# Attention with two kinds of heads and a maxout MLP on one Trainium2 core: both bias tables of the next head pair are made at the first chunk of the running pair

## The chip, the cores and the metric

The kernel runs on one core of one Trainium2 chip. The time is device microseconds of one execution. Before the change three runs gave 203.79, 204.90 and 205.48 us, with a median of 204.9 us. The execution that was profiled took 203.79 us; its span, from the first to the last instruction, is 202.0 us. TensorE had its full granted clock (1.000) all along.

The names of the engines in the profile: PE is TensorE (PEld its weight loads), DVE is VectorE, ACT is ScalarE, POOL is GpSimd, SP is SyncE, which issues nearly all DMAs here.

## The reference, cut to what matters

There are 4 batches, 8 heads, 768 positions and a head dimension of 64. Some heads ("retrieval") see every earlier position, the others see only the first 4 positions and a window of the last 64. Which is which comes as an input, `is_retrieval`. The output of the attention goes through an MLP that takes the larger of two products.

```python
scores = (1 / sqrt(64)) * q @ k.T                    # per batch and head
causal = rel >= 0                                    # rel = query position - key position
stream = causal & ((key < n_sink) | (rel < window))  # n_sink 4, window 64
mask   = causal where is_retrieval else stream       # per head
a      = softmax(where(mask, scores, -1e9))
x      = (a @ v), heads side by side                 # [4 * 768, 512]
out    = maximum(x @ w1, x @ w2) @ w_out             # d_ff 1024, output float32
```

## The kernel before, in words

**Tiling.** Two heads make a pair, and there are 4 pairs in a batch, 16 in all, numbered `n`. The scores are computed transposed, keys on the partitions. Of the 6 x 6 blocks of 128 x 128, the 21 on and below the diagonal of the causal mask are grouped in six chunks `c` (`CHUNKS`), four blocks each, but for chunk 3, which has one. A step `t` is one chunk of one pair: `n, c = divmod(t, 6)`.

**A chunk's way.** `scores(t)` lets PE multiply k by q into a PSUM tile `ps` (L279). `expo(t)` lets ACT take the exponential of both heads' blocks at once (L305), into `at`. `weighted(t)` lets PE multiply `at` by the values into `po` (L342). After chunk 1 and after chunk 5 half of the queries are complete, and `normalise` lets DVE take a reciprocal (L358) and multiply (L359) into `x`. There are two `ps` tiles, so the scores of a chunk wait until the exponential two chunks earlier is done.

**The bias tables.** Blocks near the diagonal need the mask. In the first batch (pairs 0 to 3) the mask is added to the scores: `scores` issues, after the q-k products of chunks 0 to 3, two more matmuls per chunk, one a head, that multiply the identity by a table `msk[:, h]` (L294), accumulating into `ps`. The table of head `h` is 128 x 512 bf16, and one DVE instruction makes it (`biases(h)`, L556, a scalar_tensor_tensor: `tab_a * rbig[h] + tab_n`). Its inputs are ready before the first pair starts, and nothing later overwrites what it reads. Once the first batch is over, `masks` turns the eight tables into tables of 0 and 1 (L563), and the later batches multiply the exponentials by them (L323, L327).

**Who transposes q and k.** For pair `n + 1`, the cast q and k are transposed on PE (L203, into a PSUM tile `pt`) during pair `n`: q in step 0, its PSUM tile copied to SBUF by ACT (L156); k in step 1, copied by DVE (L154, `qkt<-pt`). In step 3 the finished `x` of pair `n - 1` is transposed and copied by DVE (L154, `xt<-pt`). GpSimd casts q, k and v from float32 (L243, L189) and multiplies v by the retrieval flags (L191); then it makes half of the weight difference `w1 - w2` (L551), as soon as the DMA of `w1` has landed. DVE makes the other half after the first batch's scores.

**Order.** The schedule is written out by hand: each engine executes its instructions in the order in which the program issues them. The loop of the first batch issues, in step `t`: the scores and the exponential of step `t + 2`, the weighted sum of step `t - 1` (with `normalise` where a half is complete), side work, then the bias tables, then the pending transposes (`flush`). So the scores of the first chunk of pair `n + 1` are issued in step 4 of pair `n`; `normalise(n - 1, 1)` in step 0; the copy of k in step 1; `normalise(n, 0)` in step 2.

**After the first batch** come the MLP's first products, `relu(x @ (w1 - w2))` (L378; the kernel uses max(a, b) = b + relu(a - b)), then three more batches of attention with the MLP of the batch before mixed in by a planner (`fill`, `step`), which counts estimated TensorE time only while the program is being written. `biases` adds 0.7 to a count of DVE work, `given["v"]`, that is set to zero after the first batch. The last MLP ends the kernel (L378, L395).

Of the kernel before, what the change touches and what calls it, by code (L numbers as in the profile page):

```python
# [37 lines left out]
def kernel(  # L38
# [16 lines left out]
    HP = H // 2  # L55
# [82 lines left out]
    def vec(us):  # L138
        given["v"] += us
        return nc.vector  # L140
# [83 lines left out]
    def turn_half(n, half, bank, on_vector=True):  # L224

        b, p = pairs[n]
        w = S // 2
        pt = bank("pt").bitcast(BF16)[:, 0:w]
        for i in range(NB // 2):
            nc.tensor.transpose(  # L230
                pt[:, i * 128:(i + 1) * 128],
                st[n]["x"][:, half * NB // 2 + i].rearrange("p h d -> p (h d)"), ident,
            )
        evac(xts[b][:, p, half * w:(half + 1) * w], pt, 200, on_vector=on_vector)
# [30 lines left out]
    def scores(t):  # L265
        n, c = divmod(t, NCH)
        s = st[n]
        ps = psum_s.tile([128, 2, 512], F32, tag="ps", name="ps")
        runs = []
        for e, (j, i) in enumerate(CHUNKS[c][0]):  # L270
            if runs and runs[-1][0] == j and runs[-1][1] + runs[-1][3] == i:
                runs[-1][3] += 1
            else:
                runs.append([j, i, e, 1])
        w = len(CHUNKS[c][0])
        for j, i, e, m in runs:
            for hh in range(2):
                rows = slice(64 * hh, 64 * hh + 64)
                nc.tensor.matmul(  # L279
                    ps[:, hh, e * 128:(e + m) * 128],  # L280
                    lhsT=s["qkt"][rows, 1, j * 128:(j + 1) * 128],
                    rhs=s["qkt"][rows, 0, i * 128:(i + m) * 128],
                    start=(e == 0), stop=(e + m == w), skip_group_check=True,
                )
        if n < HP and CHUNKS[c][1] is not None:

            e, m, block, reps = CHUNKS[c][1]
            per = m // reps
            for hh in range(2):
                nb = msk[:, 2 * pairs[n][1] + hh, block:block + per, :]  # L290
                nb = nb.rearrange("p e c -> p (e c)")
                if reps > 1:
                    nb = nb.unsqueeze(1).to_broadcast([128, reps, per * 128])
                nc.tensor.matmul(  # L294
                    ps[:, hh, e * 128:(e + m) * 128], lhsT=ident, rhs=nb,
                    start=False, stop=True, skip_group_check=True,
                )
        s["ps", c] = ps

    def expo(t):  # L300
        n, c = divmod(t, NCH)
        s = st[n]
        w = 128 * len(CHUNKS[c][0])
        at = atp.tile([128, 2, 4, 128], BF16, tag="at", name="at")
        sca(0.13 + 2 * w / 1300).activation(  # L305
            out=at.rearrange("p h e c -> p h (e c)")[:, :, 0:w],
            in_=s["ps", c][:, :, 0:w], func=ACT.Exp, scale=scale,
        )
        s["at", c] = at

    def mask(t):
        n, c = divmod(t, NCH)
        what = CHUNKS[c][1]
        if what is None or n < HP:
            return
        e, m, at_block, reps = what
        h0 = 2 * pairs[n][1]
        at = st[n]["at", c][:, :, e:e + m, :]
        per = m // reps
        mk = msk[:, h0:h0 + 2, at_block:at_block + per, :]  # L320
        eng = vec(0.1 + m * 0.15)
        if reps == 1:
            eng.tensor_tensor(out=at, in0=at, in1=mk, op=ALU.mult)  # L323
        else:
            mk = mk.rearrange("p h e c -> p h (e c)").unsqueeze(2)
            at = at.rearrange("p h (g e) c -> p h g (e c)", g=reps)
            eng.tensor_tensor(  # L327
                out=at, in0=at, in1=mk.to_broadcast([128, 2, reps, per * 128]), op=ALU.mult
            )

    def weighted(t):
        n, c = divmod(t, NCH)
        s = st[n]
        at = s["at", c]
        for hh in range(2):
            for e, (j, i) in enumerate(CHUNKS[c][0]):
                half, col = divmod(i, 3)
                first = ("po", half) not in s
                if first:
                    s["po", half] = psum_o.tile([128, 2, 3, D + 1], F32, tag="po", name="po")  # L340
                rhs = s["vb"][:, hh, j, :] if i - j < 2 else s["vf"][:, hh, j, :]
                nc.tensor.matmul(  # L342
                    s["po", half][:, hh, col, :], lhsT=at[:, hh, e, :], rhs=rhs,
                    start=first, stop=(c == (LO_DONE, HI_DONE)[half]),
                    skip_group_check=True,
                )
        if c == LO_DONE:
            normalise(n, 0)
        if c == HI_DONE:
            normalise(n, 1)  # L350
# [79 lines left out]
    def spend(us):  # L430
        plan["pe"] += us
# [59 lines left out]
    def flush():  # L491
        while turns:
            run_short(turns)
# [55 lines left out]
    def diff_w(eng, e):  # L549
        cols = slice(e * QC, (e + 1) * QC)  # L550
        eng.tensor_tensor(  # L551
            out=w12[:, :, cols], in0=w1f[:, :, cols], in1=w2f[:, :, cols], op=ALU.subtract
        )

    def biases(h):
        vec(0.7).scalar_tensor_tensor(  # L556
            out=msk[:, h].rearrange("p e c -> p (e c)"), in0=tab_a, scalar=rbig[:, h:h + 1],
            in1=tab_n, op0=ALU.mult, op1=ALU.add,
        )
# [69 lines left out]
    def side(t, last, first_batch):  # L629

        n, c = divmod(t, NCH)
        b, p = pairs[n]
        m = n + 1
        if m < min(last, LONG):
            if c == (QS if first_batch else 0):
                turns.append((0.34, lambda bank: turn(m, 0, bank), 0))
            if c == (KS if first_batch else 1):
                turns.append((0.34, lambda bank: turn(m, 1, bank), 0))
        if m + 1 < last:
            if m + 1 < LONG and c == 5:  # L640
                cast_qk(m + 1, 0, nc.gpsimd if first_batch else nc.vector)
                cast_qk(m + 1, 1, nc.gpsimd)
            if m + 1 >= LONG and c == 2:
                cast_qk(m + 1, 0, nc.gpsimd)
                cast_qk(m + 1, 1, nc.gpsimd)
        if first_batch:
            if c == XS and n > 0:
                turns.append((0.34, lambda bank: turn(n - 1, None, bank), 0))
        elif c == (0 if p == 0 else 4) and n > HP:
            turn_x(n - 1)  # L650
        if m + 1 < last and m + 1 >= LONG and c == 4:
            turn_qk(m + 1)
        if c == 2 and m < last:
            cast_v(m, nc.gpsimd)
        if b > 0:
            if p == 0 and n > HP and c == 0 and n + 3 < len(pairs):
                load_pair(n + 3)
            if p < HP - 1 and c == 4 and n + 4 < len(pairs):
                load_pair(n + 4)
# [7 lines left out]
    for t in range(T0):  # L667
        if t + 2 < T0:
            scores(t + 2)
            expo(t + 2)  # L670
            spend(0.8)
        if t > 0:
            weighted(t - 1)
            spend(0.4)
        if t + 1 < T0:
            mask(t + 1)
        side(t, HP, True)
        n, c = divmod(t, NCH)
        if c in (1, 2) and n + 1 < HP:
            biases(2 * n + c + 1)  # L680
        flush()
        if t == 18:
            diff_w(nc.gpsimd, 0)
            diff_w(nc.gpsimd, 2)
        if t == 21:
            turn_half(HP - 1, 0, bank_d)
            diff_w(vec(1.2), 1)
# [11 lines left out]
    n = HP  # L699
# [43 lines left out]
    for t in range(T0, T + 2, 2):  # L743
# [12 lines left out]
        c = t % NCH  # L756
# [70 lines left out]
```

## Time and profile before

| what | us |
|---|---|
| median of three runs (lowest, highest) | 204.9 (203.79, 205.48) |
| the profiled execution | 203.79 |
| its span | 202.0 |
| PE busy / ACT busy / DVE busy / POOL busy | 184.6 / 113.8 / 109.5 / 67.6 |
| chain that ended last, share of the span: PE / ACT / DVE / DMA | 70% / 10% / 9% / 6% |
| first batch of attention, start of the first exponential to start of the first MLP product | 9.16 to 36.52 |
| bias tables (L556), 8 instructions, shortest / median / longest | 0.744 / 1.026 / 1.974 |

The profile is that of one execution. Its page gives the busy time of each engine, then the chain of work that ended last, and the groups of instructions by source line. The trace behind it gives each instruction with its start and duration, and for an engine's idle time what ended it. A busy PE says little by itself, since its matmuls are pipelined and their ends are modelled; the waits and the chain say what holds the time.

Shares over the whole span hide that the kernel has stages. PE is 91% busy over the span, but in the second and third pairs' stretches, 15.64 to 22.95 and 22.95 to 30.93 us, it was busy 5.83 us of 7.31 and 5.82 of 7.98; ACT was busy 5.78 and 5.77 in them, and DVE 4.88 and 5.57.

### The profile page before, as it was taken

The numbers are of one execution on the slowest core, as the hardware profiler recorded it, in microseconds if no ns is written. First come the engines' busy times: TensorE is split into PE (matmuls) and PEld (weight loads), VectorE is DVE, ScalarE is ACT, GpSimd is POOL, SyncE is SP. The second block draws the span as 40 slices with busy tenths as digits, with TensorE's granted clock in tenths as the row PEclk, the third lists the DMA queues.
The fourth block names the chain that finished last, engine by engine and source line by source line (L and its number), as shares of the span: only waits on it lengthen the run. The fifth ranks groups of instructions, "written<-read, shape, count | busy, mean of one in ns | idle before, by whom it ended". The sixth has DMA issues, their size and how long they took to land.

```text
span 202.0 us, 4508 instructions
## 1 busy us (share of the span) xinstructions
PE 184.6 (91%) x1844; PEld 103.8 (51%) x1869; DVE 109.5 (54%) x207; ACT 113.8 (56%) x153; POOL 67.6 (33%) x75
## 2 busy tenths in 40 slices
PE   7889768999789999979899999999999999999992
PEld 2356445667445555546446455555555645554440
DVE  1864593987657557478493847573733631432110
ACT  2598677578787785794536547926353622341111
POOL 1397368999005352424361533070200000000000
PEclk9999999999999999999999999999999999999999
DMA  6999999999943949999999999992704104100222
GB/s 209 298 290 335 387 351 303 324 328 305 220 73 75 201 110 220 223 197 232 198 256 216 212 233 230 207 185 97 170 2 124 73 0 143 55 0 0 104 104 104
DMA packets 82694, 37.35 MB, mean 185 GB/s; under 512 B 71794, under 2 KB 77938, under 8 KB 82674
## 3 DMA queue, kind: packets, MB, share of 16 engines
q1 hardware_dynamic: 82528, 36.77, 78.2%
q10 hardware_dynamic: 146, 0.30, 0.6%
q8 instruction: 14, 0.23, 0.5%
q14 instruction: 6, 0.05, 0.1%
HBM read 25.46 MB, written 6.29 MB: 157 GB/s over the span
## 4 chain that ended last, share of the span: by engine, by line
PE 70%; ACT 10%; DVE 9%; DMA 6%; issue 3%; SPq 0%; ACTq 0%
PE pout L395 27%; PE ph L378 19%; PE po L342 8%; PE ps L279 8%; ACT at L305 8%; DMA qkt<-qk 3%; PE pw L534 3%; PE pt L203 3%; DMA kn<-in_k_dram 2%; PE ps L294 2%; DVE msk L556 2%; DVE x L359 2%; DVE qkt L154 1%; DVE at L327 1%; ACT qkt L156 1%
## 5 line engine op out<-in xcount | busy, mean ns | idle before, releaser
L305 ACT ACTIVATE at<-ps 128x1024 bf16<-128x1024 f32 x96 | 83.5, 917 | 33.9 <-PE ps L279 28.1
L378 PE MATMUL ph<-xt,w 128*128 128x384 bf16 x256 | 48.3, 326 | 0.8 <-ACT ot L156 0.4
L395 PE MATMUL pout<-wob,g 128*128 128x512 bf16 x180 | 45.7, 379 | 0.6
L279 PE MATMUL ps<-qkt 64*128 64x256 bf16 (+1 forms) x416 | 30.3, 251 | 5.9 <-ACT at L305 3.7
L152 DVE TENSOR_SCALAR g<-ph 128x384 bf16<-128x384 f32 x34 | 18.9, 556 | 26.3 <-PE ph L378 26.2
L378 PEld LDWEIGHTS <-w 128*128 128x128 bf16 x256 | 23.4, 98 | 15.9 <-issue 1.7
L342 PEld LDWEIGHTS <-at 128*128 128x128 bf16 x672 | 25.0, 97 | 12.0 <-issue 9.6
L191 POOL TENSOR_TENSOR vf<-vb,rj 128x520 bf16<-128x520 bf16 x16 | 17.7, 1108 | 36.4 <-PE po L342 35.7
L395 PEld LDWEIGHTS <-g 128*128 128x128 bf16 x192 | 18.5, 98 | 20.1 <-issue 0.4
L279 PEld LDWEIGHTS <-qkt 64*128 64x128 bf16 x416 | 15.5, 94 | 23.6 <-issue 17.7
L395 PE MATMUL pout<-w2o,xt 128*128 128x512 bf16 x89 | 24.9, 378 | 0.5
L156 ACT ACTIVATE g<-ph 128x384 bf16<-128x384 f32 x30 | 14.7, 491 | 18.7 <-PE ph L378 18.7
L323 DVE TENSOR_TENSOR at<-at,msk 128x1024 bf16<-128x1024 bf16 (+2 forms) x36 | 18.6, 520 | 10.3 <-ACT at L305 10.3
L156 ACT ACTIVATE ot<-pout 128x512 f32<-128x512 f32 x9 | 5.4, 597 | 25.5 <-PE pout L395 25.5
L154 DVE COPY ot<-pout 128x512 f32<-128x512 f32 x15 | 10.3, 690 | 17.1 <-PE pout L395 16.9
L342 PE MATMUL po<-vb,at 128*128 128x65 bf16 x352 | 19.0, 194 | 0.0
L359 DVE TENSOR_TENSOR x<-po,rez 128x384 bf16<-128x384 f32 x32 | 17.8, 557 | 1.1
L342 PE MATMUL po<-vf,at 128*128 128x65 bf16 x320 | 17.9, 194 | 0.0
L243 POOL CAST qk<-qn 128x768 bf16<-128x768 f32 x10 | 8.7, 870 | 26.1 <-DMA qn<-in_q_dram 22.8
L358 DVE RECIPROCAL rez<-po 128x6 f32<-128x6 f32 x32 | 6.2, 192 | 20.2 <-PE po L342 20.0
L243 POOL CAST qk<-kn 128x768 bf16<-128x768 f32 x15 | 14.9, 992 | 5.5 <-DMA kn<-in_k_dram 4.7
L189 POOL CAST vb<-vn 128x768 bf16<-128x768 f32 x16 | 13.9, 868 | 6.8 <-DMA vn<-in_v_dram 6.8
(52 smaller groups left out, 131.7 us busy)
## 6 DMA issues: line engine op xcount, KB each, us to landing
qn<-in_q_dram SPq DMA_DIRECT2D x16, 384.0 KB, 5.5
kn<-in_k_dram SPq DMA_DIRECT2D x16, 384.0 KB, 5.6
vn<-in_v_dram SPq DMA_DIRECT2D x16, 384.0 KB, 6.5
out_dram<-ot SPq DMA_DIRECT2D x24, 256.0 KB, 2.2
w2f<-in_moe_w_dram SPq DMA_DIRECT2D x2, 1024.0 KB, 9.6
w1f<-in_moe_w_dram SPq DMA_DIRECT2D x4, 512.0 KB, 10.4
wof<-in_moe_w_out_dram SPq DMA_DIRECT2D x2, 1024.0 KB, 10.1
tab<-mask_table ACTq DMA_DIRECT2D x1, 288.5 KB, 3.5
```

What stands on the lines that cost most here:

```text
L152: eng.tensor_scalar_max(out=out, in0=in_, scalar1=0.0)
L156: sca(0.2 + cols / 1300).activation(out=out, in_=in_, func=ACT.Relu if relu else ACT.Copy)
L189: eng.tensor_copy(out=vb[:, :, :, 0:D], in_=s["vn"])
L191: nc.gpsimd.tensor_tensor(out=vf, in0=vb[:, :, 0:4, :], in1=rj[:, 2 * p:2 * p + 2, :].unsqueeze(3).to_broadcast([128, 2, 4, D + 1]), op=AL ...
L243: eng.tensor_copy(out=s["qk"][:, e], in_=src.rearrange("p h n d -> p n h d"))
L279: nc.tensor.matmul(ps[:, hh, e * 128:(e + m) * 128], lhsT=s["qkt"][rows, 1, j * 128:(j + 1) * 128], rhs=s["qkt"][rows, 0, i * 128:(i + m) ...
L305: sca(0.13 + 2 * w / 1300).activation(out=at.rearrange("p h e c -> p h (e c)")[:, :, 0:w], in_=s["ps", c][:, :, 0:w], func=ACT.Exp, scale= ...
L323: eng.tensor_tensor(out=at, in0=at, in1=mk, op=ALU.mult)
L342: nc.tensor.matmul(s["po", half][:, hh, col, :], lhsT=at[:, hh, e, :], rhs=rhs, start=first, stop=(c == (LO_DONE, HI_DONE)[half]), skip_gr ...
L359: vec(0.55).tensor_tensor(out=s["x"][:, 3 * half:3 * half + 3].rearrange("p i h d -> p h i d"), in0=po[:, :, :, 0:D], in1=rez.unsqueeze(3) ...
L378: nc.tensor.matmul(ph, lhsT=w12[:, kc, fc * 128:(fc + 1) * 128], rhs=xts[b][:, kc, tg * GT:(tg + 1) * GT], start=(kc == 0), stop=(kc == KC ...
L395: nc.tensor.matmul(pout, lhsT=lhsT, rhs=rhs, start=(e == 0), stop=(e == len(steps) - 1),)
```

## The change

In the first batch, the two tables of the next pair's heads were made in two different steps: that of its first head in step 1, that of its second head in step 2, each after the step's weighted sum and normalisation and ahead of its transposes. Now both are made in step 0, one behind the other, at the same place within the step. Six of the eight tables move so (heads 2 to 7; those of pair 0 are made before the loop). Nothing is added or removed: DVE executes the same instructions in another order, and no other engine's order changes.

```diff
         side(t, HP, True)
         n, c = divmod(t, NCH)
-        if c in (1, 2) and n + 1 < HP:
-            biases(2 * n + c + 1)
+        if c == 0 and n + 1 < HP:
+            biases(2 * n + 2)
+            biases(2 * n + 3)
         flush()
```

DVE's order from step 0 to step 3 of pair `n`, before: `normalise(n - 1, 1)`, first table, copy of k, `normalise(n, 0)`, second table, copy of `x`. After: `normalise(n - 1, 1)`, first table, second table, copy of k, `normalise(n, 0)`, copy of `x`.

## The prediction

> **What bounds the kernel now.** I started with the chain that ended last, cut to the first 50 us, because the change touches nothing later. Columns: start, us, what. Around the start of pair 2 it reads:
>
> ```profile
> 19.57 0.94 DVE qkt L154
> 20.52 0.11 DVE rez L358
> 20.63 0.02 issue
> 20.66 0.56 DVE x L359
> 21.21 1.22 DVE msk L556
> 22.43 0.04 issue
> 22.47 0.39 PE ps L294
> 22.95 1.03 ACT at L305
> ```
>
> The chain runs through DVE: copy of k, normalisation, second table; only then may PE add the bias and ACT take the exponential. The same passage ends at 15.64 (pair 1) and at 30.93 (pair 3). The table of waits for the first 45 us (total, times, longest) gives the price:
>
> ```profile
> PE ps L294 <- DVE msk L556: 3.8, 3, 1.9
> ACT at L305 <- PE ps L294: 5.5, 7, 2.0
> ```
>
> Three waits of PE for a table, one at each change of pairs: 0.60, 1.26 and 1.95 us in PE's timeline. ACT idles 0.61, 1.36 and 2.05 there. ACT's idle time between ordinary chunks is 0.17, so 0.44, 1.19 and 1.88, together 3.5 us, is the most that can be won.
>
> Next, DVE's timeline (start, us) and POOL's over the same stretch:
>
> ```profile
> 18.64 1.01 DVE L556 SCALAR_TENSOR_TENSOR msk<-tab,rbig 128x512 bf16<-128x512 bf16 x1
> 19.57 0.94 DVE L154 COPY qkt<-pt 128x768 bf16<-128x768 bf16 x1
> 21.13 1.29 DVE L556 SCALAR_TENSOR_TENSOR msk<-tab,rbig 128x512 bf16<-128x512 bf16 x1
> ...
> 25.95 1.01 DVE L556 SCALAR_TENSOR_TENSOR msk<-tab,rbig 128x512 bf16<-128x512 bf16 x1
> 28.43 1.97 DVE L556 SCALAR_TENSOR_TENSOR msk<-tab,rbig 128x512 bf16<-128x512 bf16 x1
> ```
>
> ```profile
> 18.05 1.05 POOL L191 TENSOR_TENSOR vf<-vb,rj 128x520 bf16<-128x520 bf16 x1 [1.45 <-PE po L342]
> 19.05 1.29 POOL L243 CAST qk<-qn 128x768 bf16<-128x768 f32 x1
> 21.05 0.83 POOL L189 CAST vb<-vn 128x768 bf16<-128x768 f32 x1
> 25.35 1.05 POOL L191 TENSOR_TENSOR vf<-vb,rj 128x520 bf16<-128x520 bf16 x1 [3.47 <-PE po L342]
> 27.52 2.35 POOL L551 TENSOR_TENSOR w<-w1f,w2f 128x1024 bf16<-128x1024 f32 x1 [1.11 <-DMA w1f<-in_moe_w_dram]
> ```
>
> **What a table costs.** The eight last 0.744 to 1.974 us, and one pattern explains them: a table that starts while POOL runs an instruction ends 0.53 to 0.56 after that instruction does. 18.05 + 1.05 = 19.10, and the table ends at 19.65; 21.88 and 22.42; 26.40 and 26.96; 29.87 and 30.40. With POOL idle (the first two, at 6.64) a table takes 0.744. POOL pays too: its q cast at 19.05 takes 1.29 where others take 0.82, so it ran from 19.52, 0.13 before the table's end. They take turns. The next DVE instruction starts 0.08 before its predecessor's recorded end.
>
> The Trainium skill, page "SBUF — State Buffer", section "Who interferes with whom", has the rule: a DVE instruction with two SBUF inputs and a GpSimd instruction that reads SBUF exclude each other, whoever starts first. It speaks against this change: a second table set directly behind the first meets the POOL cast that queued behind the first. A sum with 0.744 for each second table would be -2.5 us; with the turns, which the rows show as well, it is the -1.9 below.
>
> **Step by step.** From the q-k products' start to the exponential's start, with the bias ready, takes 1.03 us (16.72 to 17.75).
>
> *Into pair 1.* DVE is idle from 10.98 to 12.50, waiting for k's transpose on PE (ends 12.47). The second table is asked for at 10.90. POOL's k cast, held from 10.38, has run since 10.84 and ends at 11.66; the table ends at 11.66 + 0.55 = 12.21, inside the idle time. The copy of k stays at 12.50, so the q-k products stay at 14.17 (ACT released them), and the exponential moves from 15.64 to 14.17 + 1.03 = 15.20: **-0.44**. Cover: 0.26 us. Without it the copy may slip by another 0.6 before the products at 14.17 notice.
>
> *Into pair 2*, all 0.44 earlier. First table 18.20 to 19.21; POOL's q cast, held, 19.08 to 19.90; second table, asked for at 19.13, ends 20.45. The copy of k now queues behind it: 20.37 to 21.31, where it would have started at 19.13. This is what is late next, since the products need k. They start at 21.36, the exponential at 22.39 against 22.95: -0.56 in all, so only **-0.12** here. The normalisation, now behind k, holds nobody: its `x` is transposed a pair later, and its `po` tile is needed by the next pair only.
>
> *Into pair 3*, all 0.56 earlier. First table 25.39 to 26.40. POOL then waits until 27.52 for the `w1` DMA, issued from 17.06 on without waiting for compute, so this doesn't move. The second table, asked for at 26.32, finds the port free: 0.744, to 27.06. Copy of k 26.98 to 27.92, products 27.97, exponential 29.00 against 30.93: -1.93 in all, **-1.37** here. Before, the table came at 28.43, inside the 2.35 us weight difference, and took 1.97.
>
> Sum: 0.44 + 0.12 + 1.37 = **1.9 us** earlier at 30.93.
>
> **Bounds.** No row shows a table directly behind another while POOL is busy. At the low end, 0.744 each, the exponentials start at 15.20, 21.81 and 28.42: -2.5. At the high end, 1.97 each, at 15.20, 23.04 and 30.88: nothing gained. I take the turns, since all rows but the two with POOL idle follow them.
>
> **Does it reach the end?** From 30.93 to 36.52 ACT is busy 5.15 us of 5.59 and nothing waits for a DMA. At 36.5 the MLP starts, and PE is busy 13.46 us of the next 13.48; its start follows `x` (DVE, 35.91), which moves along. What stays put is work that a DMA or POOL holds. The first weight difference is ready at 29.87, needed at 34.6. The `w1` columns land at most 12.4 us after issues that start by 19.8, so by 32.2; DVE's differences would run at 34.7 and 37.3. POOL's chain of casts, from 30.83 on, stays where it is: the `w2` casts end about 1 us later than 37.12, since DVE's difference now falls among them, still ahead of the transposes at 41.0 (42.98 before); POOL finishes near 51 and then waits 10.6 us for PE, so it has slack. The tightest is DVE's last difference: it ends at 40.94 and its product starts at 41.19; by turns with POOL I get 39.16 and 39.25. From 62 us on, SP issues its DMAs when x tiles and casts are ready (it waited 8.5 us for the first transpose at 62.17), so those move too. I carry the whole gain: the profiled execution would go from 203.79 to 201.9, its span from 202.0 to 200.1. The same 1.9 off the median of 204.9, which is 1.1 above the profiled run, is **203.0**, 0.93% less. A measurement of this kernel can tell about 1% (2.05 us) from no change; the three runs spread by 1.7.
>
> **Rivals.**
>
> *POOL gets the port first at pair 3.* If the `w1` DMA lands by 26.3 instead of 27.5, the 2.35 us difference starts ahead of the second table, which ends near 29.2; copy, products and exponential bring 31.1. The first two steps' 0.56 is then eaten up to between 0 and 0.5: 204.4 to 204.9. For: the margin is 1.2 us, and DMA landings may vary. Against: these DMAs are issued alike in both kernels. 0.12.
>
> *Gained and given back.* The earlier stage waits later, for a POOL cast or a DMA that did not move: 204.9. For: the 0.09 us margin above, POOL busy 13.32 of 13.48 us. Against: the other margins are 1.5 us and more. 0.12.
>
> *More than the turns give.* Second tables near 0.744: 202.4. Against: six rows. 0.08.
>
> *Slower.* From 66 us on the DMA transposes of q and k share SP's queue with the loads; one at 92.06 took 6.50 us to land (median 4.0) behind 1.15 MB of loads issued from 88.97 on, and it is on the chain. If the shifted start puts two more of the eight behind loads, each 2.5 us later, that is +5.0 - 1.9: 208.0. It decides once a transpose is issued less than about 4 us after a triple of loads and PE has no other work left. Against: both are issued in SP's fixed order, after compute that moves together. 0.08.
>
> That the change doesn't do what it says would mean that the second table isn't what PE waited for; the copy of k had ended at 20.51 and the products had run at 20.82, so I give that nothing of its own.
>
> **Chances.** The forecast has 0.60, and its own range is the median's 203.0 with 0.8 either way for the runs' spread. It lies so near 1% that 0.33 of it falls beyond; with the 0.08 of the larger gain, faster is 0.41. Same: 0.27 + 0.12 + 0.12 = 0.51. Slower: 0.08. The range reaches from the low bound less the spread, 202.4 - 0.8 = 201.6, to 204.9, where the full gain is lost; the slower case and a few tails stay out.
>
> **What would show it.** PE's three waits for L556 gone, and in their place a wait for DVE's `qkt` copy of about 0.5 to 1 us before the products of pairs 2 and 3. Second tables ending 0.55 after a POOL cast in pairs 0 and 1, and 0.744 long in pair 2. First exponentials at 15.2, 22.4 and 29.0; the first MLP product near 34.6 instead of 36.52; the last stage 1.9 earlier. I am wrong if the second table of pair 2 is long again, if PE stops at 39 to 41 us for the last weight difference, or if qkt transposes land later than before.

## The result, and the profile after

The kernel after takes 202.37 us (median of six executions, 201.38 to 202.97), the kernel before 205.31 in the same measurement (203.79 to 205.53). The ratio is 0.986, with a 95% interval of 0.982 to 0.990: faster by 1.4%, 2.9 us. Two later measurements of the same kernel gave 0.9892 (0.986 to 0.992) and 0.9886 (0.986 to 0.991), so 2.2 and 2.3 us. The forecast was 203.0 us and a gain of 1.9. One execution of run r7 below, 306.05 us at a granted clock of 0.562, is slow and left out.

The chain that ended last, at the start of pair 2 (start, us, what):

```profile
19.21 1.30 DVE msk L556
20.52 0.88 DVE qkt L154
21.39 0.05 issue
21.44 0.39 PE ps L279 x4
21.83 0.16 issue
21.99 0.39 PE ps L294
22.39 0.02 issue
...
22.47 1.03 ACT at L305
```

The normalisation has left the chain. Before, it read copy of k, normalisation, table, bias matmul; now it reads table, copy of k, q-k products, bias. The waits of the first 45 us (total, times, longest) say the same:

```profile
ACT at L305 <- PE ps L294: 3.6, 7, 1.2
...
PEld L279 <- DVE qkt L154: 1.6, 2, 1.1
...
PE ps L279 <- DVE qkt L154: 1.3, 2, 0.9
```

The last two lines are those of PE's weight loads and of its matmuls. The 3.8 us of PE waiting for a table are gone. In their place PE waits for the copy of k: 0.92 us at pair 2 and 0.35 at pair 3 (PE and its weight loads wait at the same time, so the two lines aren't added). DVE's timeline shows the tables in twos:

```profile
18.28 2.24 DVE L556 SCALAR_TENSOR_TENSOR msk<-tab,rbig 128x512 bf16<-128x512 bf16 x2
20.44 0.94 DVE L154 COPY qkt<-pt 128x768 bf16<-128x768 bf16 x1
...
25.46 1.67 DVE L556 SCALAR_TENSOR_TENSOR msk<-tab,rbig 128x512 bf16<-128x512 bf16 x2
27.06 0.94 DVE L154 COPY qkt<-pt 128x768 bf16<-128x768 bf16 x1
```

and POOL's what the tables met:

```profile
18.68 1.29 POOL L243 CAST qk<-qn 128x768 bf16<-128x768 f32 x1
19.92 1.28 POOL L243 CAST qk<-kn 128x768 bf16<-128x768 f32 x1
...
27.69 2.35 POOL L551 TENSOR_TENSOR w<-w1f,w2f 128x1024 bf16<-128x1024 f32 x1 [1.77 <-DMA w1f<-in_moe_w_dram]
```

For pair 2 DVE and POOL take turns. The q cast ends at 19.97, the second table at 20.52, 0.55 later, and the k cast takes 1.28 instead of 0.82, because the table held it up in its turn. For pair 3 both tables are done at 27.13, before the weight difference starts at 27.69.

To set traces of several executions side by side, I take the time from the first exponential of pair 0 to the first MLP product ("the first batch"), and from there to the end of the span ("the rest"). The first leaves out when the first loads landed.

| kernel | first batch, us | rest, us |
|---|---|---|
| before, two traces | 27.36, 27.40 | 165.5, 165.9 |
| after, three traces | 25.44, 25.44, 25.44 | 166.1, 165.1, 165.7 |
| difference held back (r3) | 26.10 | 166.5 |
| q cast held back (r4) | 24.88 | 166.3 |
| tables of pair 3 alone (r5) | 25.99 | 166.3 |
| w1 loaded early (r6) | 29.46 | 165.7 |
| tables in DVE's idle times (r7, r10) | 24.03, 24.03 | 166.3, 166.0 |

The change shortens the first batch by 1.92 to 1.96 us, 1.94 in the middle, whichever traces are compared. The rest varies by 0.4 us between the two traces of before and by 1.1 among the three of after. Most of that arises where the chain runs through DMA landings, near 90 us. There the chain of the first trace of before, then of the first and second trace of after, reads:

```profile
92.06 6.50 DMA qkt<-qk
```

```profile
87.39 3.04 DMA qn<-in_q_dram
90.43 6.68 DMA qkt<-qk
```

```profile
87.14 3.35 DMA qn<-in_q_dram
90.49 5.88 DMA qkt<-qk
```

The same transpose, issued within 0.06 us of the same time, landed 0.7 earlier in one execution of the kernel after than in the other. That is most of why the first trace of after shows a span only 1.2 us shorter than before's, and the second one 2.3.

### The profile page after: what moved, and what is told of

Read it like the earlier page. It is cut to its first block, busy times and chain, and to the rows that moved or that the text cites. A ratio compares the mean times of both kernels' runs of the same rounds, so it can differ in the third digit from the quotient of the medians.

```text
span 200.8 us, 4508 instructions
## 1 busy us (share of the span) xinstructions
PE 184.6 (92%) x1844; PEld 103.7 (52%) x1869; DVE 108.7 (54%) x207; ACT 113.8 (57%) x153; POOL 68.4 (34%) x75
## 4 chain that ended last, share of the span: by engine, by line
PE 70%; ACT 9%; DVE 8%; DMA 7%; issue 3%; SPq 0%; ACTq 0%
PE pout L395 27%; PE ph L378 19%; PE ps L279 8%; PE po L342 8%; ACT at L305 7%; DMA qkt<-qk 3%; PE pw L534 3%; PE pt L203 3%; DMA kn<-in_k_dram 2%; PE ps L294 2%; DVE x L359 2%; DMA qn<-in_q_dram 2%; DVE qkt L154 1%; DVE msk L556 1%; DVE at L327 1%
## 5 line engine op out<-in xcount | busy, mean ns | idle before, releaser
L189 POOL CAST vb<-vn 128x768 bf16<-128x768 f32 x16 | 14.7, 918 | 7.5 <-DMA vn<-in_v_dram 7.5
```

Source lines behind the costliest of these rows:

```text
L189: eng.tensor_copy(out=vb[:, :, :, 0:D], in_=s["vn"])
```

## The experiments

The theory: the second table held up the bias of each pair's first chunk; its length came from turns with POOL; the 1.94 us won in the first batch reach the end and are all there is (theory A in the texts below). The rivals: the tables are long for a reason of their own; the change also speeds up the later stages (theory B); the early waits matter by more than their size.

**The kernel before again (r1) and the kernel after again (r2).**

> The kernel before, unchanged, for a second trace of it. Both theories of the first batch: the first MLP product starts at 36.5 us again, within 0.2. Theory A (the whole gain is made in the first batch, and what lies beyond 1.9 us is the spread of the later stages): from the first MLP product to the end of the span this trace differs from the first one's 165.5 us by 0.5 to 1.5, and the difference arises between 85 and 130 us, where the chain runs through DMA landings. Theory B (the change also speeds the later stages): this stretch is the same as in the first trace, within 0.3.

> The kernel after, unchanged, for a second trace. First MLP product at 34.7 us within 0.2. Theory A: from there to the end of the span 165 to 166 us like the kernel before (its first trace has 166.1), and the ratio to the kernel before lies near 0.988. Theory B: 164.5 or less in most executions.

Measured: 204.57 us, ratio 0.9996 (0.9968 to 1.0024), and 202.6 us, ratio 0.9892 (0.9860 to 0.9923). The traces are in the table: the first MLP product at 36.63 and 34.64, the rest 165.9 and 165.1. The rest of before differs from its first trace's by 0.4, less than the 0.5 to 1.5 expected, so r1 alone tells little; the two traces of after, 1.1 apart in the rest, are what shows the wobble.

**Is a table long because of POOL? The kernel before, with the weight difference held back (r3).**

```diff
         if c in (1, 2) and n + 1 < HP:
             biases(2 * n + c + 1)
+            if n == 2 and c == 2:
+                nc.vector.memset(w12[:, 0, 0:1], 0.0)
```

> The kernel before, with one addition: DVE writes one column of w12 directly after the second table for pair 3, so that GpSimd's first weight difference, which overwrites it, can't start before that table is made. The order of the tables stays that of the kernel before. If the table took 1.97 us because GpSimd held it up: it now takes 0.74, PE's wait for it falls from 1.95 to about 0.7, and the first MLP product and the end come 1.2 us earlier (ratio 0.994). If the table was long for a reason of its own or because of DMA writes: it still takes 1.9 to 2.0 and the time is that of the kernel before, 0 to +0.1 us.

Measured: 203.27 us, ratio 0.9932 (0.9906 to 0.9958). DVE, then POOL:

```profile
28.58 0.74 DVE L556 SCALAR_TENSOR_TENSOR msk<-tab,rbig 128x512 bf16<-128x512 bf16 x1
```

```profile
29.43 4.66 POOL L551 TENSOR_TENSOR w<-w1f,w2f 128x1024 bf16<-128x1024 f32 x2 [2.87 <-DVE w L682]
```

The same table, in the same place, takes 0.74 instead of 1.97 once POOL's instruction isn't under way, and the first batch is at least 1.26 us shorter. So POOL's instruction made it long. This alone gives more than half of what the change gives in the first batch, with no table moved.

**And behind the first table? The kernel after, with POOL's q cast held back (r4).** A one-element write by DVE into the q tile that the cast will overwrite makes the cast wait.

```diff
             biases(2 * n + 3)
+            if n + 2 < HP:
+                st[n + 2]["qk"] = work.tile([128, 2, NB, 2, D], BF16, tag="qk", name="qk")
+                nc.vector.memset(st[n + 2]["qk"][:, 0, 0, 0, 0:1], 0.0)
...
-        if e == 0:
+        if e == 0 and "qk" not in s:
```

> The kernel after, with one addition: DVE writes one element of the q tile of the pair after next directly behind the two tables, so that GpSimd's cast of that q, which overwrites it, waits until both tables are made. By the turns of DVE and GpSimd: the second table for pair 2 (19.2 to 20.5 us in the kernel after) takes 0.74, the copy of k starts near 19.95 instead of 20.44, and the first exponential of pair 2 comes at 22.0 instead of 22.47; pair 3 and the end 0.5 us earlier than in the kernel after. If the second table's 1.3 us is not GpSimd's doing: no change but +0.1 us a pair for the added write.

Measured: the two tables for pair 2 take 1.67 us together instead of 2.24, and the first batch is 0.56 shorter than after. But the time is 202.29 us, ratio 0.9882 (0.9854 to 0.9911), against 0.9892 for the kernel after beside it: 0.2 us better, with intervals of 0.6 us either way, so most of the 0.56 does not show. PE's timeline shows where it goes, then DVE's and POOL's:

```profile
34.07 1.46 PE L378 MATMUL ph<-xt,w 128*128 128x384 bf16 x8 [0.17 <-DVE xt L154]
35.37 0.41 PE L342 MATMUL po<-vf,at 128*128 128x65 bf16 x8
36.10 1.47 PE L378 MATMUL ph<-xt,w 128*128 128x384 bf16 x8 [0.32 <-DVE w L551]
```

```profile
34.20 1.84 DVE L551 TENSOR_TENSOR w<-w1f,w2f 128x1024 bf16<-128x1024 f32 x1
```

```profile
32.94 4.98 POOL L547 CAST w2b<-w2f 128x1024 bf16<-128x1024 f32 x4
```

PE's second group of MLP products waits for DVE's weight difference, which waits for POOL's second cast of w2. POOL's casts follow its own differences, and those follow the w1 DMA, so they don't move. The group starts at 36.10, 0.09 earlier than the 36.19 of the kernel after (r2), though the first group starts 0.57 earlier. The kernel after stands at the edge of this: in its first trace DVE's difference ends at 36.09 and the second group starts at 36.22.

**Do the three waits add up? The tables of pair 3 alone (r5).**

```diff
-        if c in (1, 2) and n + 1 < HP:
-            biases(2 * n + c + 1)
+        if n < 2 and c in (1, 2):
+            biases(2 * n + c + 1)
+        if n == 2 and c == 0:
+            biases(6)
+            biases(7)
```

> Only the tables of pair 3 (heads 6 and 7) move to step 0 of pair 2; those of pairs 1 and 2 stay where the kernel before has them. If the gain is the sum of three separate waits, 0.44 + 0.12 + 1.37: the first exponentials of pairs 1 and 2 stay at 15.6 and 22.95, that of pair 3 comes at 29.6 instead of 30.93, the first MLP product 1.3 to 1.4 earlier than in the kernel before, and the ratio is 0.993. If the early waits matter more than their own size: a ratio of 0.996 or more.

Measured: 203.1 us, ratio 0.993 (0.9904 to 0.9957). The first batch is 25.99, 1.37 to 1.41 less than before; the clock times are 0.46 later only because this execution started its first exponential at 9.62 instead of 9.16. So 1.37 of the 1.94 comes from pair 3 and 0.57 from the other two, the split that the steps gave.

**The first rival made to happen: the kernel after with w1 loaded early (r6).**

```diff
-    load_w(moe_w2, w2f, 0, 2)
-    load_w(moe_w2, w2f, 2, 4)
     for e in range(4):
+        load_columns(moe_w2, w2f, e)
         load_columns(moe_w1, w1f, e)
```

> The kernel after, with w2 and w1 loaded by columns in turn (w2 columns 0, w1 columns 0, w2 columns 1, ...), the same bytes in all, so that what GpSimd's first weight difference needs has landed by about 24 us instead of 27.6. This makes the prediction's first rival happen: GpSimd starts the 2.35 us difference at 25.9, ahead of the second table for pair 3. By the turns that table ends near 28.8 instead of 27.1, the first exponential of pair 3 comes at 30.7 instead of 29.1, and the first MLP product at 36.2 instead of 34.7; the end is 0.8 to 1.6 later than in the kernel after, since the later differences wait less. If the table takes the port whenever it asks: no change at 29.1.

Measured: 205.26 us, ratio 1.0028 (1.0005 to 1.0052): slower than before by 0.3%. The mechanism is the expected one, the size is larger. The traced execution took 206.39 us, the longest of twelve. DVE and POOL:

```profile
25.71 3.76 DVE L556 SCALAR_TENSOR_TENSOR msk<-tab,rbig 128x512 bf16<-128x512 bf16 x2
```

```profile
26.13 2.80 POOL L551 TENSOR_TENSOR w<-w1f,w2f 128x1024 bf16<-128x1024 f32 x1
```

POOL's difference asks while the first table runs, gets its turn when that ends, and makes the second table wait until 28.93; it ends at 29.47, not 28.8, since I had left out that the difference itself waits for the first table. The first exponential of pair 3 would then come near 31.4. It came at 32.08, and the first MLP product at 38.93 instead of 34.64, because TensorE had slowed down. PE's timeline, then busy times by stretch (the number after the five engines' is TensorE's granted clock):

```profile
30.40 0.61 PE L279 MATMUL ps<-qkt 64*128 64x256 bf16 x4 [2.45 <-DVE qkt L154]
30.94 1.03 PE L294 MATMUL ps<-msk,tab 128*128 128x512 bf16 x2
```

```profile
28.00:30.40 2.40, 0.00 (x0) 0.00 (x1) 2.40 (x3) 0.65 (x1) 1.19 (x2) 0.88 1.07 342
30.40:32.00 1.60, 1.60 (x8) 0.56 (x8) 1.07 (x3) 0.00 (x0) 1.60 (x1) 0.50 1.08 366
```

After 2.45 us without a matmul the clock is at half. A pair of 512-column bias matmuls takes 1.03 us instead of 0.60, and the windows show 0.50 until 36.5 us. Not every execution pays this: of the twelve, eight have a mean granted clock of 0.982 to 0.992 over the span and a median of 205.4 us, four have 1.000 and a median of 204.6.

**A version beyond both: tables in DVE's idle times (r7, r10), and with the difference moved too (r8).**

```diff
-        if c == 0 and n + 1 < HP:
-            biases(2 * n + 2)
-            biases(2 * n + 3)
+        if t in (0, 3, NCH + 3):
+            h = {0: 2, 3: 4, NCH + 3: 6}[t]
+            biases(h)
+            biases(h + 1)
```

> The tables of pair 1 in step 0 of pair 0 as after the change, those of pair 2 in step 3 of pair 0 and those of pair 3 in step 3 of pair 1, where DVE idles 3.4 and 2.2 us: no table is left between the normalisation and the copy of k. First exponentials at 15.25, 21.4 and 27.6 us (after: 15.25, 22.45, 29.05), the first MLP product at 33.2. What follows is limited by the weight difference on DVE, which takes turns with GpSimd's casts: if it costs little, the end is 1.3 to 1.5 earlier than in the kernel after (ratio to before 0.982); if it takes back what the first batch gains, 0 to 0.4 earlier (0.987).

Measured: 201.49 us, ratio 0.9848 (0.9819 to 0.9877). The first exponentials of pairs 2 and 3, in ACT's timeline:

```profile
21.55 1.94 ACT L305 ACTIVATE at<-ps 128x1024 bf16<-128x1024 f32 x2 [0.26 <-PE ps L294]
...
27.75 1.94 ACT L305 ACTIVATE at<-ps 128x1024 bf16<-128x1024 f32 x2 [0.26 <-PE ps L294]
```

ACT's idle time at the change of pairs falls from 1.25 and 0.68 to 0.26. The first batch is 1.41 us shorter than in the kernel after. The second group of MLP products starts at 35.16, 1.03 earlier than in r2 (1.13 counted from the first exponential): about 0.3 of the gain is taken back at the weight difference, which ends at 35.10, as in r4.

r8 moves DVE's first difference ahead, out of the way of POOL's casts of w2:

```diff
-        if t == 18:
+        if t == 17:
             diff_w(nc.gpsimd, 0)
+            diff_w(vec(1.2), 1)
             diff_w(nc.gpsimd, 2)
         if t == 21:
             turn_half(HP - 1, 0, bank_d)
-            diff_w(vec(1.2), 1)
```

> The kernel of the run before, with DVE's first weight difference issued in step 5 of pair 2 instead of step 3 of pair 3, so that it doesn't meet GpSimd's casts of w2. DVE waits for the w1 columns there (about 29.1) and for GpSimd's difference (29.95), and the normalisations behind it come up to 1.7 late, which the products that need their PSUM tile may notice by 0.6. If the difference is what holds PE near 36 us: PE's second group of MLP products starts without waiting for it and the end is 0.3 to 0.6 earlier than in the run before. If the normalisations matter more: 0 to 0.6 later.

Measured: 201.29 us, ratio 0.9845 (0.9818 to 0.9873), no different from r7. The second group no longer waits for the difference, but the normalisation behind it is late, PE waits for its PSUM tile, and the first group starts at 33.65 instead of 33.33; the second starts at 35.20 either way.

> The kernel with the tables in the idle times of DVE, once more, beside the kernel after on the same chip. Its first trace had the second group of MLP products at 35.16 us against 36.19 in the kernel after, so 0.8 to 1.1 us earlier: a ratio to the kernel before of 0.984, 0.005 below that of the kernel after. If the turns at the weight difference take it back: no more than 0.002 below.

> The kernel after, for a third trace and as the mate of the two other runs. By theory A its ratio is 0.991, by the two measurements so far 0.986 to 0.989.

Measured side by side: tables in the idle times 201.16 us, ratio 0.9827 (0.980 to 0.9853); the kernel after 202.47 us, ratio 0.9886 (0.986 to 0.9911). The intervals don't overlap: the version with the tables in DVE's idle times beats the kernel after by 0.6%, 1.3 us, and the kernel before by 1.7%.

**Does the change give more than the first batch shows? The kernel after, made late (r9).**

```diff
         first_ups.pop(0)[1]((bank_a, bank_d)[e])
+    pz2 = bank_s("pz2")
+    for _ in range(9):
+        nc.tensor.matmul(pz2, lhsT=zero[:, 0:128], rhs=zero, start=True, stop=True)
     weighted(T0 - 1)
```

> The kernel after, with nine matmuls of 512 columns on zeros (0.216 us each, 1.94 us) on TensorE behind the first two groups of MLP products, so that from there on TensorE runs at about the times of the kernel before, while the tables are made as after the change. Theory A (the change gives its 1.9 us in the first batch and nothing later): the time is that of the kernel before, ratio 0.998 to 1.002. Theory B (something later is faster as well, for the measured 2.4 to 2.9 us): the ratio stays at 0.995 or below.

Measured: 204.16 us, ratio 0.9966 (0.9948 to 0.9985), between the two. In its trace the second group of MLP products starts at 38.21 (before: 38.25 and 38.17) and the last MLP at 172.26 (before: 171.89 and 172.38), so the traced execution is one of the kernel before in all that follows. Before's median, 204.99, is 0.8 us above this; what that is, the next run shows.

**Is it the clock? The kernel before, with PE kept busy in its longest wait (r12).**

```diff
+        if n == 3 and c == 0:
+            pd = bank_a("pd")
+            for _ in range(6):
+                nc.tensor.matmul(pd, lhsT=zero[:, 0:128], rhs=zero, start=True, stop=True)
         if n < HP and CHUNKS[c][1] is not None:
```

> The kernel before, with six matmuls of 512 columns on zeros (1.3 us) on TensorE between the q-k products and the bias of pair 3's first chunk, inside its 1.95 us wait for the second table; the wait's end and everything behind it keep their times. It asks whether the idle time of TensorE costs more than its length in some executions, by a lowered clock afterwards, as it did after 2.4 us of idle time in the run with the early w1 loads. If so, the executions that cost the kernel before more than its profiled one drop out: median near 204.2, narrow, ratio 0.996 to 0.997, and that explains why the change gave 2.3 us where the first batch shows 1.9. If not: ratio 0.999 to 1.002, and the spread of the kernel before, about 0.6, stays.

Measured: 204.63 us, ratio 0.999 (0.9964 to 1.0017). The wait is filled, as PE's timeline shows; the longest wait that PE has left is the 1.26 us at pair 2:

```profile
28.85 1.24 PE L288 MATMUL pd<-zero 128*128 128x512 bf16 x5 [0.16 <-issue]
...
30.47 0.38 PE L298 MATMUL ps<-msk,tab 128*128 128x512 bf16 x1 [0.16 <-DVE msk L560]
```

By the median alone the answer would be no. But the mean granted clock of each execution (the share of the full clock that TensorE got) is on record too, and it falls into two groups with nothing between them: 0.988 to 0.992 ("lowered"; 0.982 once, in r6), and 0.996 to 1.000 ("full").

| kernel | executions | lowered | median lowered, us | median full, us |
|---|---|---|---|---|
| before, in the four later measurements and r1 | 81 | 45 | 205.26 | 204.23 |
| before, PE kept busy (r12) | 12 | 0 | | 204.63 |
| after (first measurement, r2, r11) | 18 | 0 | | 202.51 |
| r3, r4, r5, r7, r8, r9, r10 | 47 | 0 | | |
| w1 loaded early (r6) | 12 | 8 | 205.44 | 204.57 |

So it is the clock. More than half of the executions of the kernel before on record run with a lowered clock and take 1.0 us longer. They are gone when nothing but the 1.95 us wait at pair 3 is filled: none of 12 in r12, 7 of 17 for the kernel before beside it. No kernel in which that wait is shorter has one. The ratios of r3 and r5, taken against all executions of before, contain a part of this. Both traces of before, and that of r12, are of full-clock executions, so where the clock falls in a lowered one, and for how long, is not shown; r12 shows what sets it off.

The median of r12 didn't drop to 204.2 as expected. Its slow end did: the longest execution took 204.86 us, that of the kernel before beside it 205.99. But its full-clock executions have a median of 204.63, the ten of the kernel before 204.25. Both sets spread over 1.3 to 1.7 us and their means differ by 0.2, so that may be chance; the trace shows nothing that would make r12 longer (first batch 27.17, rest 165.8).

This also settles r9. Of the kernel before beside it, the six full-clock executions have a median of 204.35 us; r9, always at full clock, has 204.16. The late kernel after is the kernel before at full clock, as theory A says, and its missing 0.7 us are lowered executions that it doesn't have.

## Why the prediction was right

The forecast of 203.0 us was 0.6 above the measured median, which lies within the range. The likeliest single case, within 1%, did not come: the gain is 1.1 to 1.4%. Point by point:

- **Into pair 1**, -0.44: the exponential came at 15.28 (15.20 forecast; this trace's first exponential came 0.07 later than before's). Both tables fitted into DVE's idle time, of which 0.33 us were left.
- **Into pair 2**, -0.12: 22.47, forecast 22.39. The second table ended at 20.52, forecast 20.45, and the copy of k was what came late.
- **Into pair 3**, -1.37: 29.09, forecast 29.00. POOL was idle as expected; the two tables took 1.67, which is 1.01 and 0.74 with the usual overlap of 0.08.
- **The turns** were right, and r3 and r4 show them as the cause of the long tables. What the Trainium skill says of DVE and GpSimd on the page "SBUF — State Buffer", section "Who interferes with whom", agrees with them: 0.74 against 1.97 us for one table. The sum of -2.5 us without turns would have missed the first batch's 1.94 by 0.6.
- **The way to the end** was right in its order of margins. The tightest place named, the weight differences on DVE, is where r4's further half microsecond was lost. The prediction saw it at the last difference; in r4 PE waits 0.32 for the first one of DVE.
- **The first rival**, POOL starting ahead of the second table, happens once r6 loads `w1` earlier, but was mis-sized: 204.4 to 204.9 by its working, 205.26 measured. It left out the difference's own wait for the first table (the second table ended at 29.47 in r6, against its 29.2) and TensorE's lowered clock after the longer gap.
- **The slower rival** did not come. The q and k transpose it named landed 5.9 to 6.7 us after its issue in all three traces of after, against 6.5 in both of before.

What the prediction had wrong, inside its range, is the base from which it took the 1.9 us. It read the 1.1 us by which the median lay above the profiled execution as spread of the runs, and carried them unchanged to the kernel after. The profiled execution had the full clock, "all along" as the text ahead of the prediction says; 45 of 81 later ones did not. Their 1.0 us hangs on the wait at pair 3, which the change removes, so the change wins twice: the wait itself in every execution, and the lowered clock in about half of them. Full clock against full clock the medians are 204.23 and 202.51 us, a gain of 1.7 (1.5 on the chip of r2, 1.9 on that of r11), by which the 1.94 us of the first batch do reach the end. Over all executions it is 2.2 to 2.9. In the first measurement four of the six executions of before took 205.27 to 205.53 us, where the lowered ones lie elsewhere; their clock is not on record, so that the 2.9 comes from them is likely and not shown.

That the forecast came within 0.6 us is thus in part luck. Full clock against full clock its base was 0.7 too high (204.9 for 204.23) and its gain 0.2 too large; had the three runs at hand been lowered ones, at 205.3, it would have said 203.4.

## What to carry to other kernels

Look at what stands between a stalled instruction and the engine that stalls it: here a table without any dependence was queued behind a copy and a normalisation, and that order, with GpSimd's instruction beside the late table, was the stall. Put such work where its engine idles for another reason, not only earlier; the version that did so won 1.3 us more. Before moving a DVE instruction that takes turns with GpSimd, lay GpSimd's timeline beside it, and place it by the end of the GpSimd instruction it will meet, not by its mean duration. And before adding a gain to a median, ask whether the profiled execution is like the median one: here the granted clock of each execution would have shown that it was not.

## What was new of the hardware

- A gap in TensorE's work of 2.45 us was followed by half the clock (0.50) from before 30.4 to about 36.5 us (r6). Gaps of 1.95 and 1.70 us in the two traced executions of the kernel before left it at 1.00; but in 45 of 81 executions of that kernel the mean clock was 0.988 to 0.992, and filling this one gap left 0 of 12 (r12). So in this kernel a gap of about 2 us costs clock in some executions and not in others. The Trainium skill, page "TensorE: Matmul & The Clock Gate", section "What's actually happening", puts the fall after an idle window of about 3.4 us that runs freely; here shorter gaps were enough, and the measurement decides.
- DVE and POOL hand over in turns in these traces: when both have an instruction ready, each waits for the one of the other engine that asked before it, and both sides lose, the table 0.57 us and the cast 0.46 (pair 2, after).
